# An explicit order list, row-pair projections and a new layout of the casts in a fused attention and mixer kernel

## The chip, the cores and the metric

The kernel runs on one core of one Trainium2 chip. The metric is the device time of one execution in microseconds, given as the median of several runs; the profiler's span of one execution is about 2 us shorter. TensorE does the matmuls and transposes, VectorE and ScalarE the elementwise work, GpSimd some scaling and the issue of transfers that convert types, SyncE the issue of other transfers. Sixteen DMA engines carry all transfers.

## The reference

Linear attention with positive features feeds an MLP mixer. There are 8 batches, 8 heads, 576 tokens of 64 elements per head, 128 features, and mixer widths of 256 (tokens) and 1536 (channels). Cut to what matters:

```python
def phi(x):                                   # x is q or k, scaled
    h = np.einsum('bhsd,md->bhsm', x, omega) - np.sum(x * x, axis=-1, keepdims=True) / 2.0
    return np.exp(h - np.max(h, axis=-1, keepdims=True)) / np.sqrt(m)
q_p, k_p = phi(q_s), phi(k_s)                 # the "projections"
kv = np.einsum('bhsm,bhsd->bhmd', k_p, v)
num = np.einsum('bhsm,bhmd->bhsd', q_p, kv)   # divided by q_p times the sum of k_p: x
h = np.maximum(xt @ w_tok1, 0.0) @ w_tok2     # token mixing; u = x + h
h2 = np.maximum(u @ w_ch1, 0.0) @ w_ch2       # channel mixing; out = u + h2
```

## The kernel before

All operands of the matmuls are fp16 in on-chip memory. TensorE needs q, k and u with their columns on the partitions. For batches 0 and 1, TensorE itself transposes q and k. For batches 2 to 7 the path is longer: a transfer issued by GpSimd casts the fp32 q or k to a scratch array in memory (`cast_dram`), and a DMA transpose issued by SyncE reads it back (`load_T`). The transposes of u are matmuls on TensorE in all batches.

```python
    def cast_dram(b, which):
        src = q if which == "q" else k
        t = dpool.tile([H * SP2, 2 * D], FP16, name=f"{which}16", tag=f"{which}16")
        nc.gpsimd.dma_start(
            out=t.rearrange("(a x) y -> a (x y)", a=P),                     # 128 rows of 4.5 KB
            in_=src[b].rearrange("h (e s) d -> (h e) (s d)", e=P // H),
        )
        live[which + "16", b] = t
    ...
    def q_proj(b, hp, w):          # one of 2 matmuls: all 128 rows, half of them zero in bd
        nc.tensor.matmul(ps, bd[:, w * M : (w + 1) * M], sb[:, 2 * hp : 2 * hp + 2, 0:NP2], ...)
    ...
    def u_transpose(src, dst):     # 4 transposes on TensorE, one copy on VectorE
        ps = mix_ps([P, ND, P], FP16, "uT_ps")
        for db in range(ND):
            nc.tensor.transpose(ps[:, db, :], src[:, db * P : (db + 1) * P], ident16)
        nc.vector.tensor_copy(out=dst, in_=ps)
    ...
    for _, _, fn, args in sorted(steps, key=lambda s: s[:2]):   # order by places in time
        fn(*args)
```

The order of the steps fixes the order on each engine: where one step waits, those behind it on that engine wait too (9.6 us on TensorE in a case below). Each `ps` is a bank of the matmul accumulator (PSUM): three for attention, two for `kv`/`num`, three for the mixer.

The softmax here doesn't subtract the row's maximum and nothing guards it: scores larger than these inputs give would overflow.

Of the kernel before, what the change touches and what calls it, by code (L numbers as in the profile page):

```python
# [17 lines left out]
def kernel(  # L18
# [43 lines left out]
    def att_ps(shape, dt, name):  # L62
        return pspool.tile(shape, dt, name=name, tag="attps", bufs=3)
# [4 lines left out]
    def mix_ps(shape, dt, name):  # L68
        return pspool.tile(shape, dt, name=name, tag="mixps", bufs=3)
# [5 lines left out]

    def cast_dram(b, which):

        src = q if which == "q" else k
        t = dpool.tile([H * SP2, 2 * D], FP16, name=f"{which}16", tag=f"{which}16")
        nc.gpsimd.dma_start(  # L80
            out=t.rearrange("(a x) y -> a (x y)", a=P),
            in_=src[b].rearrange("h (e s) d -> (h e) (s d)", e=P // H),
        )
        live[which + "16", b] = t
# [8 lines left out]
    def load_v(b):  # L93

        if b < 2:
            t = ldpool.tile([P, H, NJ, D], FP16, name="v_16", tag="v_16", bufs=2)
            live["v", b] = t
            nc.gpsimd.dma_start(
                out=t.rearrange("p h j d -> p h (j d)"),
                in_=v[b, :, 0:SM, :].rearrange("h (p j) d -> p h (j d)", j=NJ),  # L100
            )
            return
        t = ldpool.tile([P, H, NJ, D], FP32, name="v_nat", tag="v_nat", bufs=2)
        live["v", b] = t
        for e in range(2):
            nc.sync.dma_start(
                out=t[:, :, 2 * e : 2 * e + 2, :].rearrange("p h w d -> p h (w d)"),
                in_=v[b, :, e * NP2 : (e + 1) * NP2, :].rearrange("h (p w) d -> p h (w d)", w=2),
            )

    def load_v_tail(b):
        t = ldpool.tile([P, 4, D], FP32, name="v_tail", tag="v_tail", bufs=2)
# [27 lines left out]
    def cast_qk(which):  # L140
        nc.vector.tensor_copy(out=live[which + "nat", 0][:, 0:2, :], in_=stage[which])
# [9 lines left out]
    warm = xt[0]  # L151
    nc.vector.memset(warm, 0.0)
    for b in range(2):
        new_nat(b)
# [5 lines left out]
    make_identity(nc, ident16)  # L160
    load_nat(0, 2, 4, "q")
    load_nat(0, 2, 4, "k")
    load_nat(0, 4, 8, "q")
    load_nat(0, 4, 8, "k")
    load_nat_tail(0, "k")
    load_nat_tail(0, "q")
    load_v(0)
# [5 lines left out]
    omega_nat = wpool.tile([P, 2 * D], FP16, name="omega_nat")  # L173
    nc.vector.tensor_copy(out=omega_nat[:, 0:D], in_=om_f)
    nc.vector.tensor_copy(out=omega_nat[:, D : 2 * D], in_=om_f)

    bd = wpool.tile([P, 2 * M], FP16, name="bd")
    nc.vector.memset(bd, 0.0)
# [11 lines left out]

    om_ps = att_ps([P, P], FP16, "om_ps")
# [3 lines left out]

    nc.vector.memset(w1t, 0.0)

    def clear_vz():
        for t in vz:
            nc.vector.memset(t, 0.0)  # L200

    def clear():
        nc.vector.memset(w2t, 0.0)
        nc.vector.memset(xt[1], 0.0)
        for t in q_pt:
            nc.vector.memset(t[:, 0:ST], 0.0)
            nc.vector.memset(t[:, SM + ST : SM + 2 * ST], 0.0)
# [10 lines left out]
    def permute_w2():  # L218
        for tb in range(NT):
            nc.vector.tensor_copy(  # L220
                out=w2m[:, tb], in_=w2raw[:, tb, 0:SM].rearrange("p (c j) -> p j c", j=NJ)
            )
            nc.vector.tensor_copy(out=w2t[:, tb, 0, 0:ST], in_=w2raw[:, tb, SM:S])
            nc.vector.tensor_copy(out=w2t[:, tb, 1, ST:P], in_=w2raw[:, tb, SM:S])
# [15 lines left out]
    steps = []  # L240

    def at(place, fn, *args):
        steps.append((place, len(steps), fn, args))


    def t_main(b, h0, n, which):

        if h0 == 0:
            live[which + "T", b] = ldpool.tile(
                [P, H, SP2], FP16, name=f"{which}T", tag=f"{which}T", bufs=2  # L250
            )
        ps = att_ps([P, n, 2, P], FP16, "t_ps")
# [5 lines left out]
        copy = nc.vector.tensor_copy if which == "q" else nc.scalar.copy  # L258
        copy(  # L259
# [4 lines left out]
    def t_tail(b, which):  # L264
# [4 lines left out]
        nc.vector.tensor_copy(out=live[which + "T", b][:, :, NP2:SP2], in_=ps)  # L269
# [32 lines left out]
    def k_tail_max(b, eng):  # L302
# [8 lines left out]
        for hh in range(4):  # L311
# [3 lines left out]
            eng.tensor_tensor(  # L315
# [6 lines left out]
    def q_proj(b, hp, w):  # L322
        sb = live["qT", b]
        if w == 0:
            live["qp", b, hp] = apool.tile([P, 2, 2, 2, P], FP16, name="q_p", tag="q_p", bufs=3)
        ps = att_ps([P, 2, NP2], FP32, "q_ps")
        nc.tensor.matmul(  # L327
            ps, bd[:, w * M : (w + 1) * M], sb[:, 2 * hp : 2 * hp + 2, 0:NP2], start=True, stop=True
        )
        how = "m i (e p) -> m i e p" if b < 2 else "m i (p e) -> m i e p"  # L330
        exp(live["qp", b, hp][:, w], ps.rearrange(how, e=2))

    def k_proj(b, hp, i):
        sb = live["kT", b]
        if i == 0:
            live["kp", b, hp] = apool.tile([P, 2, 4, M], FP16, name="k_p", tag="k_p", bufs=3)
        ps = att_ps([P, 4, M], FP32, "k_ps")
        for e in range(2):
            nc.tensor.matmul(  # L339
                ps[:, 2 * e : 2 * e + 2, :],  # L340
                sb[:, 2 * hp + i, e * P : (e + 1) * P],
                bd,
                start=True,
                stop=True,
            )
        exp(live["kp", b, hp][:, i], ps)

    def k_max(b, hp, eng):
# [9 lines left out]
        with nc.allow_low_precision(reason="fp16 operand of the matmul"):  # L358
            nc.vector.reciprocal(out=vs[:, :, D], in_=mx)
        eng.tensor_tensor(  # L360
# [6 lines left out]
    def kv(b, hp):  # L367
        ps = kn_ps([P, 2, D + 1], FP32, "kv_ps")
        kp, vs = live["kp", b, hp], live["vsc", b, hp]
        for i in range(2):  # L370
            for j in range(NJ):
                nc.tensor.matmul(  # L372
                    ps[:, i, :], kp[:, i, j, :], vs[:, i * 4 + j, 0 : D + 1], start=(i + j == 0), stop=False
# [11 lines left out]
        nc.scalar.copy(out=sb, in_=ps)  # L385
        live["kv", b, hp] = sb

    def num(b, hp, i):
# [3 lines left out]
        sb = live["kv", b, hp][:, i, :]  # L392
        ps = kn_ps([P, NJ, D + 1], FP32, "num_ps")
# [42 lines left out]
    def tok1(b, tb):  # L436
# [10 lines left out]
        if tb == 0:  # L447
# [29 lines left out]
    def u_transpose(src, dst):  # L477
# [3 lines left out]
        nc.vector.tensor_copy(out=dst, in_=ps)  # L481

    def tokT(b, j):
        if j == 0:
            live["uT", b] = mpool.tile([P, ND, NJ, P], FP16, name="uT", tag="uT")
        u_transpose(live["u", b][:, j, :], live["uT", b][:, :, j, :])
# [39 lines left out]
    L = {"dram2": 1.8, "wc2": 0.001, "dram": 2.766, "T": 2.8, "klo": 1.017, "khi": 3.57, "clo": 4.0, "klo0": 1.094, "khi0": 3.57, "clo0": 4.0, "wc1": 1.85}  # L526
    O = {"qt": -0.334, "kt": 0.472, "ktm": 1.279, "q0": 0.018, "q1": 0.449, "k0": 0.207, "k1": 0.468, "km": 0.711, "kv": 1.426, "num": 1.72, "dn": 0.204, "norm": 1.74, "nt": 2.248}
    O0 = {"qt": 2.914, "kt": 0.685, "ktm": 1.13, "q0": 0.018, "q1": 0.525, "k0": -0.372, "k1": 0.182, "km": 0.711, "kv": 1.426, "num": 1.72, "dn": 0.204, "norm": 1.74, "nt": 2.248, "tq": -0.681, "tk": -0.669, "tail": 0.327}
    O1 = {"qt": 2.914, "kt": 0.685, "ktm": 1.13, "q0": -0.375, "q1": 0.613, "k0": 0.06, "k1": 0.182, "km": 0.711, "kv": 1.426, "num": 1.72, "dn": 0.219, "norm": 1.74, "nt": 2.248, "tq": -0.681, "tk": -0.669, "tail": 0.285}
    def load_second():  # L530
        load_wtok()
        load_nat(1, 0, 4, "q")
        load_nat(1, 0, 4, "k")
        load_nat(1, 4, 8, "q")
        load_nat(1, 4, 8, "k")
        load_nat_tail(1, "k")
        load_nat_tail(1, "q")
        load_v(1)
        load_v_tail(1)

    at(-0.97, cast_qk, "q")
    at(-0.96, cast_qk, "k")
    at(-0.90, load_second)
    at(L["dram2"], cast_dram, 2, "q")
    at(L["dram2"], cast_dram, 2, "k")
    at(L["wc1"], load_wc1, 0)
    at(L["wc1"], load_wc1, 1)
    for part in range(2):
        at(8 + O["kt"] + L["wc2"], load_wc2, part)
    at(0.05, clear_vz)  # L550
    at(0.95, clear)
    at(2.95, permute_w2)
    for b in range(2):
        n = 2 if b == 0 else 4
        o = (O0, O1)[b]
        for h0 in range(0, H, n):
            at(4 * b + h0 / 2 + o["tq"], t_main, b, h0, n, "q")
            at(4 * b + h0 / 2 + o["tk"], t_main, b, h0, n, "k")
        at(4 * b + o["tail"], t_tail, b, "k")
        at(4 * b + o["tail"] + 0.001, t_tail, b, "q")  # L560

    def load_T_v(b):
        for which in "qk":
            load_T(b, which)
        load_v(b)
        load_v_tail(b)

    for b in range(2, B):
        if b > 2:
            for which in "qk":  # L570
                at(4 * (b - 2) + L["dram"], cast_dram, b, which)
        at(4 * (b - 2) + L["T"], load_T_v, b)

    for b in range(B):
        o = (O0, O1)[b] if b < 2 else O
        g = 4 * b
        at(g + o["qt"], q_tail, b)
        at(g + o["kt"], k_tail, b)
        at(g + o["ktm"], k_tail_max, b, nc.gpsimd if b else nc.vector)
        for hp in range(NU):  # L580
            u = g + hp
            at(u + o["q0"], q_proj, b, hp, 0)
            at(u + o["q1"], q_proj, b, hp, 1)
            at(u + o["k0"], k_proj, b, hp, 0)
            at(u + o["k1"], k_proj, b, hp, 1)
# [62 lines left out]
```

## Time and profile before

| | before |
|---|---|
| time, median of 3 runs (range) | 321.0 us (320.54 to 321.78) |
| span of the profiled execution | 318.9 us |
| first channel-mixing matmul | 48.1 us |
| TensorE lost before it / after it | 26.1 us / 2.1 us |
| after the last matmul | 4.8 us |

"Lost" is the time in which TensorE streams nothing that the result needs. The prediction below shows the lines for these. The profile also has the list of DMA issues: how often, how large, and the median time from the issue to the landing in us. For the kernel before:

```profile
q<-in_q_dram POOLq DMA_DIRECT2D x6, 576.0 KB, 7.6
k<-in_k_dram POOLq DMA_DIRECT2D x6, 576.0 KB, 10.2
qT<-q SPq DMA_TRANSPOSE x6, 6.9
```

The first two rows are the six casts of q and of k, the last the six transposes of q.

### The profile page before, as it was taken

The page shows a single profiled execution, that of the slowest core. Times are in us where ns is not written, and L with a number is a line of the kernel's source. Part 1 is how long each engine was busy: PE and PEld are TensorE (multiplying, and loading weights), DVE is VectorE, ACT ScalarE, POOL GpSimd, SP SyncE. Part 2 cuts the span into 40 slices and gives each one's busy share as a digit, 9 for nine tenths or more (in the row PEclk, how much of TensorE's full clock was granted, in tenths as well). Part 3 has the DMA queues.
Part 4 walks back from the last instruction along what each step waited for, and adds up shares of the span by engine and source line. Part 5 has one row for each costly group of instructions (what it writes and reads, how often), then busy time and mean ns, then how long its engine had stood idle before and what let it go on. Part 6 is the DMA issues. An engine that isn't in the chain of part 4 may idle for free.

```text
span 318.9 us, 5525 instructions
## 1 busy us (share of the span) xinstructions
PE 299.3 (94%) x2137; PEld 159.1 (50%) x2137; DVE 173.8 (55%) x463; ACT 155.8 (49%) x299; POOL 71.6 (22%) x102
## 2 busy tenths in 40 slices
PE   5657889999999999999999999999999999999993
PEld 1435455555555555555555555555555444444441
DVE  3599996567455745674558456755385244002011
ACT  1557668633673367416842684358523610440610
POOL 9550535402141214121412131112311000000000
PEclk9598999999999999999999999999999999999998
DMA  7999999999990699059905991110011001002014
GB/s 150 195 195 211 192 244 213 196 238 205 153 256 35 128 173 244 25 123 175 259 3 128 158 238 54 68 66 2 1 67 68 0 27 74 33 2 102 30 39 92
DMA packets 59689, 38.75 MB, mean 121 GB/s; under 512 B 31120, under 2 KB 54544, under 8 KB 59280
## 3 DMA queue, kind: packets, MB, share of 16 engines
q1 hardware_dynamic: 48736, 24.16, 32.4%
q0 software_dynamic: 10656, 13.99, 26.2%
q8 instruction: 16, 0.26, 0.3%
q10 hardware_dynamic: 272, 0.26, 0.3%
q14 instruction: 9, 0.07, 0.1%
HBM read 35.88 MB, written 16.52 MB: 164 GB/s over the span
## 4 chain that ended last, share of the span: by engine, by line
PE 81%; DVE 10%; DMA 3%; POOL 3%; issue 1%; ACT 0%; POOLq 0%; DVEq 0%
PE h_ps L507 29%; PE h_ps L495 28%; PE ht_ps L457 4%; PE k_ps L339 3%; PE q_ps L327 3%; PE h_ps L441 3%; DMA v<-in_v_dram 3%; PE uT_ps L480 2%; PE num_ps L396 2%; PE kv_ps L372 2%; DVE xm L405 1%; PE kv_ps L377 1%; DVE km L355 1%; PE htt_ps L468 1%; POOL vz L315 1%
## 5 line engine op out<-in xcount | busy, mean ns | idle before, releaser
L507 PE MATMUL h_ps<-wc,r 128*128 128x512 f16 x432 | 98.1, 379 | 0.0
L502 ACT ACTIVATE r<-h_ps 128x512 f16<-128x512 f32 x108 | 64.8, 600 | 58.4 <-PE h_ps L495 56.2
L495 PE MATMUL h_ps<-uT,wc 128*128 128x512 f16 x384 | 93.0, 379 | 0.2 <-DVE uT L481 0.2
L507 PEld LDWEIGHTS <-r 128*128 128x128 f16 x432 | 41.0, 98 | 45.8
L495 PEld LDWEIGHTS <-wc 128*128 128x128 f16 x432 | 40.9, 98 | 41.3 <-issue 0.5
L360 POOL TENSOR_TENSOR v_sc<-v_nat,v_sc 128x512 f16<-128x512 f32 x24 | 25.4, 1058 | 130.5 <-DVE rc L404 91.4
L272 ACT ACTIVATE q_p<-q_ps 128x512 f16<-128x512 f32 x64 | 38.0, 599 | 33.1 <-PE q_ps L327 33.0
L516 DVE TENSOR_TENSOR o_sb<-um,h_ps 128x512 f32<-128x512 f16 x32 | 22.0, 688 | 48.0 <-PE h_ps L507 47.6
L272 ACT ACTIVATE k_p<-k_ps 128x512 f16<-128x512 f32 x64 | 37.8, 598 | 2.8 <-PE k_ps L339 1.5
L351 DVE TENSOR_TENSOR mx<-k_p 128x512 f16<-128x512 f16 x32 | 13.6, 425 | 37.0 <-ACT k_p L272 37.0
L405 DVE TENSOR_TENSOR xm<-num_ps,rc 128x256 f16<-128x256 f32 x64 | 27.1, 424 | 2.2
L385 ACT CAST kv_sb<-kv_ps 128x130 f16<-128x130 f32 x32 | 8.5, 266 | 39.1 <-PE kv_ps L377 39.0
L327 PE MATMUL q_ps<-qT,bd 128*128 128x512 f16 x64 | 24.9, 395 | 1.6 <-DVE qT L259 1.6
L339 PE MATMUL k_ps<-bd,kT 128*128 128x256 f16 x128 | 25.1, 282 | 0.9 <-ACT kT L259 0.9
L460 DVE TENSOR_TENSOR um<-xm,ht_ps 128x512 f16<-128x512 f16 x32 | 21.7, 683 | 4.0 <-PE ht_ps L457 3.9
L355 DVE TENSOR_REDUCE km<-mx 128x8 f16<-128x512 f16 x32 | 21.9, 686 | 1.1
L396 PEld LDWEIGHTS <-q_p 128*128 128x128 f16 x256 | 16.0, 99 | 10.5 <-issue 0.3
L315 POOL TENSOR_TENSOR vz<-v_tail,vz 32x256 f16<-32x256 f32 x28 | 17.3, 616 | 17.0 <-DVE vz L314 15.4
L457 PE MATMUL ht_ps<-r,w2m 128*128 128x512 f16 x64 | 19.0, 379 | 0.2
L396 PE MATMUL num_ps<-kv_sb,q_p 128*128 128x65 f16 x256 | 17.9, 195 | 0.1
L339 PEld LDWEIGHTS <-kT 128*128 128x128 f16 x128 | 12.1, 100 | 10.6 <-ACT kT L259 1.7
L441 PE MATMUL h_ps<-xm,w1m 128*128 128x512 f16 x64 | 16.4, 379 | 0.0
(93 smaller groups left out, 270.7 us busy)
## 6 DMA issues: line engine op xcount, KB each, us to landing
out_dram<-o_sb SPq DMA_DIRECT2D x32, 256.0 KB, 2.4
v_nat<-in_v_dram SPq DMA_DIRECT2D x12, 512.0 KB, 5.7
q<-in_q_dram POOLq DMA_DIRECT2D x6, 576.0 KB, 7.6
k<-in_k_dram POOLq DMA_DIRECT2D x6, 576.0 KB, 10.2
wc<-in_moe_w_ch_dram POOLq DMA_DIRECT2D x4, 768.0 KB, 14.9
v_tail<-in_v_dram SPq DMA_DIRECT2D x32, 32.0 KB, 4.7
v<-in_v_dram POOLq DMA_DIRECT2D x2, 512.0 KB, 8.6
out_dram<-o_sb SPq DMA_DIRECT2D x8, 128.0 KB, 2.3
```

What stands on the lines that cost most here:

```text
L272: nc.scalar.activation(out=out, in_=in_, func=AF.Exp, bias=0.0, scale=c_scale)
L327: nc.tensor.matmul(ps, bd[:, w * M : (w + 1) * M], sb[:, 2 * hp : 2 * hp + 2, 0:NP2], start=True, stop=True)
L339: nc.tensor.matmul(ps[:, 2 * e : 2 * e + 2, :], sb[:, 2 * hp + i, e * P : (e + 1) * P], bd, start=True, stop=True,)
L355: nc.vector.reduce_max(out=mx, in_=tmp, axis=AX.X)
L360: eng.tensor_tensor(out=vs[:, :, 0:D], in0=live["v", b][:, 2 * hp : 2 * hp + 2].rearrange("p h j d -> p (h j) d"), in1=vs[:, :, D : D + 1] ...
L396: nc.tensor.matmul(ps[:, j, :], live["qp", b, hp][:, j % 2, i, j // 2, :], sb, start=True, stop=True)
L405: nc.vector.tensor_tensor(out=live["x", b][:, :, h * D : (h + 1) * D], in0=ps[:, :, 0:D], in1=rc.unsqueeze(2).broadcast_to((P, NJ, D)), op ...
L441: nc.tensor.matmul(ps, w1m[:, j, tb * P : (tb + 1) * P], live["x", b][:, j, :], start=(j == 0), stop=False)
L457: nc.tensor.matmul(ps, w2m[:, tb, j, :], live["r1", b][:, tb, :], start=(tb == 0), stop=(tb == NT - 1))
L495: nc.tensor.matmul(ps, wc1[:, db, cb * P : (cb + 1) * P], uT[:, db].rearrange("p j c -> p (j c)"), start=(db == 0), stop=(db == ND - 1),)
L502: nc.scalar.activation(out=live["r3", c][:, cb, :], in_=ps, func=AF.Relu)
L507: nc.tensor.matmul(ps, live["r3", c][:, cb, j * P : (j + 1) * P], wc2[:, cb, :], start=(cb == 0), stop=(cb == NCB - 1),)
```

## The change

The stated intent: one explicit order list for all steps, weights ahead of batch 2, the first channel chunk moved up, row-pair projections, zero matmuls in early gaps. The diff, cut to its core:

```diff
     def att_ps(shape, dt, name):
-        return pspool.tile(shape, dt, name=name, tag="attps", bufs=3)
+        return pspool.tile(shape, dt, name=name, tag="attps", bufs=4)
     def mix_ps(shape, dt, name):
-        return pspool.tile(shape, dt, name=name, tag="mixps", bufs=3)
+        return pspool.tile(shape, dt, name=name, tag="mixps", bufs=2)
+    HEAT = {('kv', 0, 0): 3, ('kv', 0, 1): 2, ... }      # cut: 49 zero matmuls in 16 places
 # ... cut: SWAP, which moves some copies between VectorE and ScalarE
     def cast_dram(b, which):
-            out=t.rearrange("(a x) y -> a (x y)", a=P),
-            in_=src[b].rearrange("h (e s) d -> (h e) (s d)", e=P // H),
+            out=t.rearrange("(a n x) y -> n a (x y)", a=4 * H, n=9),
+            in_=src[b].rearrange("h (e n s) d -> n (h e) (s d)", e=4, n=9),
+    def heat(ps, *key):
+        for _ in range(HEAT.get(key, 0)):
+            nc.tensor.matmul(ps, warm[:, 0:P], warm, start=True, stop=True)
 # ... cut: order of the first loads; w2's permutation and tail scaling to GpSimd
-    def q_proj(b, hp, w): ...
-    def k_proj(b, hp, i): ...
+    def proj(b, hp):
+        rows = [slice(w * D, (w + 1) * D) for w in range(2)]
+        om = [bd[rows[w], w * M : (w + 1) * M] for w in range(2)]
+        heat(kps[0], "proj", b, hp)
+        for t in range(4):
+            for w in range(2):
+                nc.tensor.matmul(kps[w][:, t, :],
+                    kT[rows[w], 2 * hp + t // 2, (t % 2) * P : (t % 2 + 1) * P], om[w], ...)
+        for w in range(2):
+            nc.tensor.matmul(qps[w], om[w], qT[rows[w], 2 * hp : 2 * hp + 2, 0:NP2], ...)
+    def u_write(b, j):          # u of batches 2 to 7 and the tails to memory
+        nc.sync.dma_start(out=live["u16", b][j * P : (j + 1) * P, :], in_=src)
+    def load_uT(b):             # and back, transposed
+        for db in range(ND):
+            nc.sync.dma_start_transpose(out=dst[:, db]..., in_=live["u16", b][:, db * P : (db + 1) * P])
-    L = {"dram2": 1.8, ... }    # cut: all places in time and the sort over them
+    order = """
+        load_nat_tail 1 k; load_nat 1 0 4 k; load_nat 1 0 4 q; cast_qk k; cast_qk q; t_main 0 0 2 k; ...
+        num_tail 0 0; t_main 1 4 4 k; permute_w2 0; kv 0 3; num 0 3 1; load_T_v 2; proj 1 1; ...
+        1; t_main 1 4 4 q; norm 0 3 0; load_v_all 2; num_tail 0 1; tok1 0 0; ...
+    """                         # cut: 81 lines
```

One part of the diff is in no word of the intent: the layout of the casts. The scratch array holds the same bytes afterwards, but the transfer now goes over 9 groups of 32 pieces of 2 KB, with the 9 outermost, where it went over 128 pieces. (Another edit that no word names: the tail of v has one buffer in place of two. SyncE waits up to 8.9 us for it after the change, but also 9.4 us in the fastest kernel of the study, so it isn't what separates them.)

## The prediction

> **What bounds the kernel now.** I read the page's busy shares first, then the span in slices, then the busy time per stretch, then the chain that ended last, and at the end the TensorE groups by shape. The page, parts 1 and 2:
>
> ```profile
> span 318.9 us, 5525 instructions
> ...
> PE 299.3 (94%) x2137; PEld 159.1 (50%) x2137; DVE 173.8 (55%) x463; ACT 155.8 (49%) x299; POOL 71.6 (22%) x102
> ...
> PE   5657889999999999999999999999999999999993
> ...
> DVE  3599996567455745674558456755385244002011
> ...
> PEclk9598999999999999999999999999999999999998
> DMA  7999999999990699059905991110011001002014
> ```
>
> One slice is 8 us. TensorE is full from the seventh slice (48 us) to the end. Before that it is not, its clock dips twice, VectorE is the full engine and the DMA engines are full too. The busy time per stretch (columns: stretch, length, busy PE, PEld, DVE, ACT, POOL, each with its count, then granted clock, DMA share and GB/s) says the same in numbers:
>
> ```profile
> 10.00:20.00 10.00, 5.72 (x58) 3.61 (x57) 7.18 (x26) 5.40 (x11) 5.57 (x8) 0.71 1.39 198
> 20.00:30.00 10.00, 7.49 (x84) 5.18 (x85) 9.55 (x29) 7.07 (x14) 2.07 (x4) 0.83 1.37 222
> 40.00:50.00 10.00, 8.80 (x89) 5.29 (x87) 9.43 (x26) 6.78 (x14) 2.72 (x5) 1.00 1.18 250
> 90.00:120.00 30.00, 30.00 (x222) 16.32 (x221) 17.99 (x48) 15.88 (x32) 6.97 (x11) 1.00 0.65 145
> ```
>
> So there are two stages. Up to about 48 us VectorE is the bound (9.4 to 9.6 of 10 us) on data that is still arriving; after it TensorE has no hole at all and nothing but fewer TensorE cycles helps. The chain in order of time (start, length, what) gives the pitch of a stream of matmuls and both ends of the second stage:
>
> ```profile
> 39.81 0.44 PE k_ps L339 x4
> 46.62 0.40 PE uT_ps L480 x4
> 47.27 0.77 DVE uT L481 x2
> 48.08 1.02 PE h_ps L495 x4
> ...
> 272.63 10.36 PE h_ps L495 x48
> ...
> 314.11 0.69 DVE o_sb L516
> ```
>
> 48 matmuls in 10.36 us is 0.216 us for one of 512 columns, though the group list shows 379 ns for it (its end includes the pipeline's drain). Start to start in the trace, back to back, I find 0.216 (512 columns), 0.109 (256), 0.0555 (128), 0.058 (130) and 0.030 us (65). Multiplying each group's count by its pitch gives the work that TensorE must stream: 287.6 us, of which 1.7 is warming. The 285.9 us left, with 4.8 us after the last matmul (314.1 to 318.9), leave 28.2 us lost. The first channel matmul starts at 48.1 us, and the list of instructions has 22.0 us of useful streaming before it: 26.1 us are lost there, 2.1 us in the remaining 266 us.
>
> **What the Trainium skill says.** Row pairs: "TensorE: Matmul & The Clock Gate", Part 3, says that matmuls on different row groups run concurrently in the array, and gives 3.07 times for four; "TensorEngine Tiling (Array Packing)", Gotcha 1, adds that row tiles must write different PSUM banks, which explains why the change gives each half its own bank. The trace before has no paired tiles, so it can't confirm it. The same tiling page, Key Properties, says that changing the tiling mode drains TensorE. Here the trace has something: the 32-row transposes of the tails. Weight loads in the timeline:
>
> ```profile
> 30.43 0.24 PEld L268 LDWEIGHTS <-natt 32*128 32x128 f16 x7 [0.22 <-issue]
> 30.70 0.10 PEld L372 LDWEIGHTS <-k_p 128*128 128x128 f16 x1
> ```
>
> The seven 32-row loads follow each other every 0.025 us; the last starts at about 30.58, and the next load, of 128 rows, only at 30.70. It agrees: about 0.1 us for a switch. On the clock, the first page, Part 1, says that idling about one window of 3.4 us halves the clock; the records here show half clock at 9.0 to 15.9 and 22.7 to 26.1 us, a multiple of that window, so I believe that filler matmuls can hold it.
>
> **The change, part by part.**
>
> *Projections.* 64 query matmuls of 512 columns and 128 key matmuls of 256 become 64 of 512 and 256 of 128, on 64 rows each, in pairs.
>
> ```profile
> L339 PE MATMUL k_ps<-bd,kT 128*128 128x256 f16 x128 | 25.1, 282 | 0.9 <-ACT kT L259 0.9
> L327 PE MATMUL q_ps<-qT,bd 128*128 128x512 f16 x64 | 24.9, 395 | 1.6 <-DVE qT L259 1.6
> L480 PE MATMUL uT_ps<-ident,um 128*128 128x128 f16 x128 | 12.2, 219 | 0.8 <-DVE um L460 0.6
> ```
>
> Before: 64 x 0.216 + 128 x 0.109 = 27.8 us. After, if a pair costs one: 32 x 0.216 + 128 x 0.0555 = 14.0 us. Saved: 13.8. Against it, each of the 32 groups enters and leaves the 64-row mode: 2 x 0.1 us, 6.4 us in all; the eight groups of batches 0 and 1 lie mostly in gaps, so I charge 24 of them, 4.8 us. For imperfect overlap inside pairs I choose 1.5 us (0.05 a group).
>
> *Transposes of u.* 144 before, 32 after (batches 0 and 1 only); the others go to memory and come back by DMA transposes. Saved on TensorE: 112 x 0.0555 = 6.2 us. VectorE also loses 28 copies.
>
> So the streaming work after is 285.9 - 13.8 - 6.2 + 4.8 + 1.5 = 272.2 us.
>
> *The early stage.* I summed VectorE's and ScalarE's work ahead of the first channel chunk from the two instruction lists with the durations of the trace. VectorE: about 42 us before; after about 31 (batch 0's tail scaling, half its v scaling and the w2 permutation go to GpSimd, several copies to ScalarE, memsets into its idle start). ScalarE: at most 29 before (busy time up to 50 us), after about 33, because it takes those copies and the chunk is preceded by the same exponentials (0.60 us each). The full engine thus changes: 33 us of ScalarE from about 5.5 us (first data) at the 86% that VectorE reached before ((42 - 6) / (48 - 6), an estimate) is 44 us, and in front of the first channel chunk stand only 18.2 us of useful streaming (projections are cheaper): 25.8 us lost. At 95% it would be 40.2 and 22.0. I choose 24.5, a gain of 1.6 us. The 49 zero matmuls (10.6 us at full clock) fill gaps, and I count nothing for them beyond the held clock that these numbers need.
>
> *Loads.* Before, batch 0 and the token weights are the first 2.06 MB (fp16 bytes, by shape) of GpSimd's queue. After, batch 1's q and k and half of w_ch1 are queued ahead of the token weights: 3.96 MB, which the rate of the trace (this queue's packets bring 0.2 MB per us from about 5 us on) has in at about 26 us. The first token matmul can't run before that, and by ScalarE's sum not before about 33. It should be hidden.
>
> *PSUM.* Projections get four banks, the mixer falls from three to two. ScalarE starts 0.42 us after the start of a channel chunk's last matmul and takes 0.60; the same bank is wanted 1.08 us after that start if three chunks follow each other. The slack is 0.06 us, so each exponential that stands before such an eviction can stall TensorE for up to 0.6. The order list spreads the chunks between other matmuls; ScalarE has 44 us for 40 us of TensorE work at the beginning, but only 4 to 8 per 8 us later. I choose 4 us for all later stalls, against 2.1 before.
>
> Sum: 24.5 lost early + 272.2 + 4 + 4.8 after the last matmul = 305.5 us of span. The time is 2.1 us above the span before (321.0 against 318.9): 307.6. I shade it to 306, since the order list looks fitted to such waits.
>
> **Rivals.**
> 1. *The pairs do not overlap.* For it: the trace before shows no such pair, and both halves need their own weight load, which must then load beside the other half's matmul. Against: the skill's measured figure. It gives back 13.8 - 1.5: about 318, within 2%.
> 2. *ScalarE or the two mixer banks become the bound later.* For it: 0.06 us of slack, and TensorE's time per batch shrinks while the exponentials do not. Against: 173 us of ScalarE in all, about 57% of the new span. With 0.3 us lost at each of 30 chunks, 9 us instead of 4: 311.
> 3. *The way through memory is too slow.* A write landed in 2.4 us before, a large transpose held the queue for 3.1 and landed in 6 to 7. I expect 8 us from the last token matmul to the transposed tile. The list leaves 12.3 to 23 us of TensorE work there. It should be hidden. Batch 5's q and k have the thinnest margin: 12.4 us of work from the cast to the first use, where the cast took 5 to 12 before. One such miss costs 3 us: 309.
> 4. *The early stage gains more*, with ScalarE near 95% full: 303; and mode switches hidden as well: 299.
>
> **Range and chances.** All good terms together give 298, rivals 2 and 3 together 314. I take 298 to 315 for 8 in 10. Faster by over 2% needs a time below 314.6; only the pairs failing, or two rivals at once, prevent it: 0.86. Within 2%: 0.13. Slower: 0.01.
>
> **What would show it.** Right: the projection pairs start a few ns apart, 128-column key pairs at a pitch near 0.056 us; u's transposes fall to 32; the first channel matmul near 42 us; the clock at 1.00 from about 8 us on; TensorE idle after 50 us below 5 us. Wrong: key halves at 0.0555 each in turn (pairs serial); gaps well over 0.1 us at the edges of a projection; TensorE waiting for the relu of a channel chunk, or for DMA transposes of u, q or k; the first channel matmul still at 48 us.

## The result, and the profile after

| | before | after |
|---|---|---|
| time, median (range), 4 runs each | 320.77 us (320.40 to 321.78) | 337.85 us (336.16 to 338.84) |
| span of the profiled execution | 318.9 us | 334.4 us |
| mean granted clock | 0.980 | 0.968 |
| first channel-mixing matmul | 48.1 us | 45.3 us |

The change made the kernel 5.2% slower: the ratio is 1.0522, with a 95% interval of 1.0469 to 1.0575. Here and below a ratio is the mean time of one kernel's fast runs over that of the other's fast runs of the same rounds, so not quite the ratio of the medians quoted. Executions over 1.5% slower than the fastest of the same kernel are left out of the means.

The page after, parts 1 and 2 (busy time and share of each engine; then tenths busy in 40 slices, of 8.4 us here):

```profile
span 334.4 us, 5703 instructions
...
PE 300.0 (90%) x2202; PEld 147.7 (44%) x2202; DVE 160.6 (48%) x418; ACT 157.6 (47%) x305; POOL 81.3 (24%) x115
...
PE   6897999809999079999999999999999999999994
...
PEclk9999999976999669999999999999999999999999
```

The first six slices are better filled than before, and from the sixteenth on the row is full, as before. What is new are two holes in the row of TensorE, in the ninth and the fourteenth slice, and a lower clock in and after each. In the time per stretch (same columns as in the prediction) they are plain:

```profile
60.00:70.00 10.00, 6.01 (x26) 2.43 (x25) 6.00 (x14) 1.83 (x4) 0.00 (x0) 1.00 1.28 183
70.00:80.00 10.00, 5.03 (x53) 3.75 (x53) 1.99 (x6) 1.65 (x5) 4.49 (x6) 0.54 0.62 139
90.00:120.00 30.00, 20.18 (x159) 9.93 (x156) 13.94 (x38) 13.54 (x28) 7.32 (x10) 0.86 1.03 126
```

The stretch of 90 to 120 us was the one with 30.00 us of TensorE before; now it has 20.18. GpSimd did nothing from 60 to 70 us, and in the 5 us from 67 to 72 the four compute engines together were busy for 0.04 us, which points at a transfer. The view of waits names it (engine, line waited at, releaser: us in total, times, longest):

```profile
PE qt_ps L281 <- DMA qT<-q: 10.8, 3, 9.6
PE kv_ps L388 <- POOL v_sc L374: 7.8, 2, 7.0
```

TensorE waits 9.6 us for one DMA transpose of q. The 7.0 us wait for GpSimd is a transfer too: GpSimd's own row in the timeline shows that it waited for v of batch 2.

```profile
72.19 2.07 POOL L374 TENSOR_TENSOR v_sc<-v_nat,v_sc 128x512 f16<-128x512 f32 x2 [17.72 <-DMA v_nat<-in_v_dram]
```

The chain that ended last, in order of time (start, length, what), has these transfers as its longest pieces, and its shares by engine changed from 81% TensorE and 3% DMA to 60% and 24%:

```profile
52.87 20.11 DMA v_tail<-in_v_dram
...
100.02 18.65 DMA qT<-q
...
137.41 12.51 DMA qT<-q
```

And the rows of the DMA issues that answer to those of before:

```profile
q<-in_q_dram POOLq DMA_DIRECT2D x6, 576.0 KB, 11.7
k<-in_k_dram POOLq DMA_DIRECT2D x6, 576.0 KB, 13.0
qT<-q SPq DMA_TRANSPOSE x6, 10.3
```

A cast of q takes 11.7 us where it took 7.6, a transpose of q 10.3 where it took 6.9. Same bytes, same number.

I made a count of TensorE's gaps for all kernels: the time by which the start of each matmul lies later than the pitch of the one before it allows, if that is over 50 ns. It is 24.3 us before and 46.1 after. Up to 50 us it fell (22.4 to 13.0, with the zero matmuls counted as work); the rest is 11.6 us at 60 to 82 us, 11.3 at 108 to 123, and about 10 elsewhere.

### The profile page after: what moved, and what is told of

It is laid out like the page before. It is cut to its first block, busy times and chain, and to the rows that moved or that the text cites. A ratio compares the mean times of both kernels' runs of the same rounds, so it can differ in the third digit from the quotient of the medians.

```text
span 334.4 us, 5703 instructions
## 1 busy us (share of the span) xinstructions
PE 300.0 (90%) x2202; PEld 147.7 (44%) x2202; DVE 160.6 (48%) x418; ACT 157.6 (47%) x305; POOL 81.3 (24%) x115
## 4 chain that ended last, share of the span: by engine, by line
PE 60%; DMA 24%; DVE 4%; SPq 4%; POOL 3%; ACT 3%; issue 1%; POOLq 0%; DVEq 0%
PE h_ps L542 23%; PE h_ps L530 20%; DMA qT<-q 11%; DMA v_tail<-in_v_dram 7%; DMA v<-in_v_dram 4%; PE ht_ps L475 3%; SPq L124 2%; PE h_ps L459 2%; PE k_ps L338 2%; PE num_ps L414 2%; PE kv_ps L388 2%; DMA natt<-in_k_dram 1%; PE q_ps L346 1%; SPq L115 1%; POOL vz L318 1%
## 5 line engine op out<-in xcount | busy, mean ns | idle before, releaser
L542 PE MATMUL h_ps<-wc,r 128*128 128x512 f16 x432 | 97.1, 379 | 0.2 <-ACT r L537 0.2
L530 PE MATMUL h_ps<-uT,wc 128*128 128x512 f16 x384 | 94.1, 381 | 0.6 <-DVE rc L422 0.4
L530 PEld LDWEIGHTS <-wc 128*128 128x128 f16 x432 | 39.9, 98 | 43.3 <-issue 4.0
L551 DVE TENSOR_TENSOR o_sb<-um,h_ps 128x512 f32<-128x512 f16 x32 | 21.9, 686 | 49.4 <-PE h_ps L542 49.3
L275 ACT ACTIVATE q_p<-q_ps 128x512 f16<-128x512 f32 x64 | 36.8, 603 | 17.8 <-PE q_ps L346 17.8
L423 DVE TENSOR_TENSOR xm<-num_ps,rc 128x256 f16<-128x256 f32 x64 | 27.2, 425 | 2.2
L318 POOL TENSOR_TENSOR vz<-v_tail,vz 32x256 f16<-32x256 f32 x32 | 20.0, 623 | 29.1 <-DVE vz L317 14.3
L422 DVE RECIPROCAL rc<-num_ps 128x4 f32<-128x4 f32 x64 | 10.9, 171 | 23.5 <-PE num_ps L414 23.3
L475 PE MATMUL ht_ps<-r,w2m 128*128 128x512 f16 x64 | 20.2, 403 | 0.6 <-ACT r L537 0.5
L388 PE MATMUL kv_ps<-v_sc,k_p 128*128 128x65 f16 x256 | 13.5, 196 | 7.9 <-POOL v_sc L374 7.8
L414 PEld LDWEIGHTS <-q_p 128*128 128x128 f16 x256 | 14.9, 100 | 11.9 <-issue 3.2
L388 PEld LDWEIGHTS <-k_p 128*128 128x128 f16 x256 | 12.1, 100 | 16.1 <-issue 9.6
## 6 DMA issues: line engine op xcount, KB each, us to landing
q<-in_q_dram POOLq DMA_DIRECT2D x6, 576.0 KB, 11.7
```

Source lines behind the costliest of these rows:

```text
L275: nc.scalar.activation(out=out, in_=in_, func=AF.Exp, bias=0.0, scale=c_scale)
L318: nc.gpsimd.tensor_tensor(out=vs[r, hh, :, 0:D], in0=live["vt", b][r], in1=vs[r, hh, :, D : D + 1].broadcast_to((32, 4, D)), op=ALU.mult,)
L388: nc.tensor.matmul(ps[:, i, :], kp[:, j % 2, 2 * i + j // 2, :], vs[:, i * 4 + j, 0 : D + 1], start=(i + j == 0), stop=False)
L414: nc.tensor.matmul(ps[:, j, :], live["qp", b, hp][:, j % 2, i, j // 2, :], sb, start=True, stop=True)
L423: nc.vector.tensor_tensor(out=live["x", b][:, :, h * D : (h + 1) * D], in0=ps[:, :, 0:D], in1=rc.unsqueeze(2).broadcast_to((P, NJ, D)), op ...
L475: nc.tensor.matmul(ps, w2m[:, tb, j, :], live["r1", b][:, tb, :], start=(tb == 0), stop=(tb == NT - 1))
```

## The experiments

The theory: the casts in the new layout take longer, the transfers behind and beside them (the transposes on SyncE's queue and v behind those) land late, and TensorE waits for them. The rivals: the order list issues something in a wrong place (v of batch 2, casts of batches 4 and 5); the pairs do not overlap; the zero matmuls or the way of u through memory cost time. In all these runs the outputs were correct, and the kernel before took 320.7 to 321.1 us (medians).

### The old layout in the changed kernel

```diff
-            out=t.rearrange("(a n x) y -> n a (x y)", a=4 * H, n=9),
-            in_=src[b].rearrange("h (e n s) d -> n (h e) (s d)", e=4, n=9),
+            out=t.rearrange("(a x) y -> a (x y)", a=P),
+            in_=src[b].rearrange("h (e s) d -> (h e) (s d)", e=P // H),
```

> The changed kernel with the casts of q and k to memory in the layout of before (packets of 18 KB in place of 2 KB), nothing else. If the small packets of the new layout made casts and DMA transposes slow beside each other, the landing of qT of batch 4 (18.65 us from 100.0 us on) falls below 12 us and the time falls by some 10 us to about 328. If what matters is only that a cast is in flight beside a transpose or a load on the hardware queue, the stalls at 66 and 109 us stay within 3 us and the time stays at 335 to 341; larger packets could even make the small ones of the transposes wait longer.

Measured: 314.37 us (312.05 to 317.48), ratio 0.9765 (0.9707 to 0.9823). These two lines alone are worth 23 us, over twice what I expected. TensorE's waits for qT fell from 10.8 to 2.5 us, and the wait for v of batch 2 is gone:

```profile
PE qt_ps L281 <- DMA qT<-q: 2.5, 1, 2.5
```

The run changes the size of the pieces together with their grouping; the runs with 16 and 12 groups below part the two. Since the interval reaches across 0.98, faster by 2% is not settled by this run.

### The new layout in the kernel before

```diff
-            out=t.rearrange("(a x) y -> a (x y)", a=P),
-            in_=src[b].rearrange("h (e s) d -> (h e) (s d)", e=P // H),
+            out=t.rearrange("(a n x) y -> n a (x y)", a=4 * H, n=9),
+            in_=src[b].rearrange("h (e n s) d -> n (h e) (s d)", e=4, n=9),
```

> The kernel before with only the new layout of the casts (9 x 32 rows of 1024 elements). If the layout alone makes casts hold part of the DMA engines for long, before also gets slower: the casts' landing rises from 7.6 and 10.2 us to over 12, TensorE gets waits for qT or kT after 50 us, and the time rises by 5 to 20 us, to 326 to 341. If the layout hurts only together with the changed order and the extra DMA transposes of u, before stays within 2% (below 327).

Measured: 336.08 us (334.73 to 336.77), ratio 1.0476 (1.0443 to 1.0508). The layout slows the old kernel by about as much as the whole change did, with the same kinds of waits:

```profile
PE kv_ps L372 <- POOL v_sc L360: 6.5, 1, 6.5
PE k_ps L339 <- DMA kT<-k: 3.1, 1, 3.1
```

So the layout needs neither the order list nor anything else of the change to do its harm. It is the cause of the loss; the rest of the change, by the run before, gains.

### The number of outermost groups: 16 and 12 instead of 9

The pieces stay at 2 KB and every byte goes where it went; only the number of groups changes.

```diff
-            out=t.rearrange("(a n x) y -> n a (x y)", a=4 * H, n=9),
-            in_=src[b].rearrange("h (e n s) d -> n (h e) (s d)", e=4, n=9),
+            out=t.rearrange("(a n x) y -> n a (x y)", n=16, x=8),      # 12 in the other run
+            in_=src[b].rearrange("h s d -> (h s) d").rearrange("(a n s) d -> n a (s d)", n=16, s=16),
```

> The changed kernel with casts of the same 2 KB packets, but the outermost dimension of the copy is 16 in place of 9 (16 x 18 x 1024). If what hurts is that an outermost dimension of 9 leaves part of the 16 DMA engines out, this is as good as the old layout: 312 to 318. If what hurts is the small packets, it stays at 330 to 340.

> The changed kernel with the casts' outermost dimension 12 (12 x 24 x 1024), packets of 2 KB as with 9 and 16. If the outermost dimension sets how many of the 16 DMA engines a cast uses, the busy sum of the DMA engines during a cast alone is about 12 (it was 8 to 10 with 9 and 16 to 18 with 16), and the time lies between 310.5 and 337.9, at 313 to 326. If only a multiple of 16 helps and everything else is as bad as 9: 330 or more.

Measured with 16: 310.45 us (309.90 to 311.29), ratio 0.9685 (0.9654 to 0.9715), the fastest kernel. With 12: 327.14 us (323.32 to 331.03), ratio 1.0095 (1.0065 to 1.0125) from its two fast runs of 323.32 and 324.31; its profile fell on one of the two slow ones. The order 9, 12, 16 gives the ratios 1.0522, 1.0095, 0.9685.

The packets in the trace show why. Adding up the durations of all packets of the casts in stretches of 1 us in which little else runs gives the mean number of engines at work for a cast alone: 6.3 to 10.0 with 9 groups (93 to 98 us of that run), 12.4 to 13.2 with 12 (up to 14.5 later in the run), 16.6 to 17.9 with 16 (over 16 because packets overlap), and 16.1 to 16.2 in the kernel before. A packet of 2 KB took 172 to 173 ns (median) in all three layouts, so the packets are not slower; fewer run side by side. In bytes that is 74 to 104 KB per us with 9 groups and 154 to 203 with 16.

The records hold two more signs of it. First, GpSimd's queue has 3248 packets of 4 bytes with 9 groups, 1712 with 12 and 560 with 16. Per cast that is 224 and 96 more than with 16, just 7 x 32 and 4 x 24: one for each piece on each engine that the groups leave out. Second, two casts issued back to back fill the engines and then leave a tail. In the kernel before with the new layout each later pair of casts ran on 16 to 18 engines (by the same sum) for some 5 us and then on about 2.2 for some 4 us more (97 to 100 us, 129 to 133 and so on). This fits an estimate: two casts of nine shares each over 16 engines leave two engines with a second share, and 32 packets of 172 ns take 5.5 us. No record names the engine, so that they are the same two is inferred.

The profile of the kernel with 16 groups, the same stretches as above:

```profile
60.00:70.00 10.00, 9.62 (x98) 5.26 (x97) 9.30 (x24) 3.83 (x9) 3.47 (x5) 1.00 1.12 195
70.00:80.00 10.00, 10.00 (x78) 5.08 (x77) 5.66 (x16) 4.25 (x9) 3.07 (x4) 1.00 0.76 206
```

The hole is closed and the clock stays at 1.00. Its casts land in 8.0 and 8.3 us:

```profile
q<-in_q_dram POOLq DMA_DIRECT2D x6, 576.0 KB, 8.0
k<-in_k_dram POOLq DMA_DIRECT2D x6, 576.0 KB, 8.3
```

Longer casts would do less harm if other transfers ran at full speed beside them. They don't. In the changed kernel about two engines (1.9) were at work on casts at 109 to 112 us, and the packets of the transposes beside them took 204 to 215 ns on the mean, 85 to 104 of them per us. At 113 us, in a pause of the cast (112.5 to 113.8 us), they took 18 ns and 1022 came in one us; at 116 to 119 us, beside seven engines of the cast, they were back at 143 to 154 ns. Beside another such tail at 70 to 72 us none began at all, and the 18 in flight took 3.2 to 3.4 us each.

That a badly spread cast slows the transposes more than a well spread one is not shown. What differs plainly is how long they meet: after 18 us, DMA transposes ran beside at least one engine's worth of GpSimd's transfers for some 35 us in the changed kernel, and for 6 us with 16 groups. Why two engines hold up sixteen, these runs do not show.

### Mending by the order list: v of batch 2 earlier, casts of batch 4 and 5 closer together

```diff
-  ... num 0 3 1; load_T_v 2; proj 1 1; ... norm 0 3 0; load_v_all 2; num_tail 0 1; ...
+  ... num 0 3 1; load_T 2 q; load_v_all 2; load_T 2 k; proj 1 1; ... norm 0 3 0; num_tail 0 1; ...
```

> The changed kernel with batch 2's v loads issued between the two DMA transposes of batch 2 (at about 42.7 us, where the DMA moves only 81 GB/s) in place of behind both (48.5 us, together with w_ch2 and the casts of batch 3). Collision theory: v and its tail land before 60 us, the wait of TensorE at 66 us (7.1 + 1.9 us) and the half-clock stretch at 70.9 us go, time down by 9 to 13 us, to 325 to 329. Rival, that the DMA engines are simply short of bytes at that stage: another load (kT of batch 2, w_ch2) comes late instead and TensorE waits for that, time unchanged within 3 us.

Measured: 338.95 us (337.10 to 343.42), ratio 1.0544. The wait moved and grew, as the rival said. (The 81 GB/s in the expectation I find in no view. From 42.7 to 48.5 us the trace has 103 GB/s at a DMA share of 1.26, so few bytes moved, but the engines were not free.) The waits of TensorE:

```profile
PE k_ps L338 <- DMA kT<-k: 11.2, 1, 11.2
PE qt_ps L281 <- DMA qT<-q: 10.2, 3, 8.9
```

v now comes in time, k of batch 2 does not, and TensorE waits for it from 52.9 to 64.1 us. The second edit:

```diff
-  ... num 2 2 0; cast_dram 4 q; num 2 3 0; ... k_max 3 0; cast_dram 4 k; num_tail 2 1; ...
+  ... num 2 2 0; cast_dram 4 q; cast_dram 4 k; num 2 3 0; ... k_max 3 0; num_tail 2 1; ...
-  ... kv 3 0; cast_dram 5 q; proj_exp 3 1 0; ... proj 4 1; cast_dram 5 k; ...
+  ... kv 3 0; proj_exp 3 1 0; ... proj 4 1; cast_dram 5 q; cast_dram 5 k; ...
```

> The changed kernel with the cast of k of batch 4 issued right behind that of q, and that of q of batch 5 moved later, next to that of k. Collision theory: no cast is in flight beside the transposes of batch 4, qT of batch 4 lands in under 8 us in place of 18.65, the wait at 108.8 us (9.7 us) shrinks below 3 us with its half-clock stretch, time down by 7 to 12 us, to 326 to 331. If the transposes are slow for another reason (their number, the write-backs), the wait stays above 7 us.

Measured: 331.79 us (330.07 to 333.07), ratio 1.0337. The 9.6 us wait at 109 us is gone, but waits of 4.4 us at 138 and 2.4 at 209 came, and that for v of batch 2 stayed (6.6 us). Of the 17 us lost, this edit brings 6. Order was a partial remedy for the second hole, no cause: with the layout mended, both places in the list are harmless as they stand.

### The pairs, alone

```diff
-        rows = [slice(w * D, (w + 1) * D) for w in range(2)]
+        rows = [slice(0, P) for w in range(2)]
```

With this the two halves use all 128 rows (zeros in one half of the weights) and run one after the other, in the same order list. It was run on the changed kernel and, later, on the kernel with 16 groups.

> The changed kernel with every projection matmul on all 128 rows (the zero half of the block-diagonal omega included), so neither pairs nor a change of tiling mode; order, banks and all else as changed. If pairs run concurrently and a switch costs 0.1 us: TensorE's streaming grows by 13.8 us and the switches' 6.4 go, so up to 7 us slower where TensorE is the bound, less while it waits for DMA: 339 to 346. If the pairs are what slows the changed kernel (mode switches, bank conflicts), it gets faster, below 334.

> The changed kernel with the casts' outermost dimension 16 (310.45 us) and every projection matmul on all 128 rows: no pairs, no change of tiling mode. If pairs run concurrently and a switch costs about 0.1 us as predicted, this is slower by 13.8 - 6.4 = 7 us or a little more: 316 to 320. If the switches eat the gain: within 2 us of 310.5.

Measured: 341.36 us (339.91 to 342.06), ratio 1.0632, against 1.0522 of the changed kernel; on the mended one 315.81 us (315.05 to 316.13), ratio 0.9842 (0.9821 to 0.9863), against 0.9685. The pairs are worth 5.4 us by the medians (5.0 by the ratios) where TensorE is the bound, 3.5 where it waits for transfers anyway. The timeline of the changed kernel shows one projection of each kind, and that they overlap:

```profile
97.62 0.40 PE L338 MATMUL k_ps<-bd,kT 64*128 64x128 f16 x8
97.85 0.38 PE L346 MATMUL q_ps<-qT,bd 64*128 64x512 f16 x2
98.17 0.20 PE L414 MATMUL num_ps<-kv_sb,q_p 128*128 128x65 f16 x1
```

From the first of eight key matmuls of 128 columns to the query matmuls it is 0.23 us (one after the other, at the pitch of 0.0555, 0.44), and the two query matmuls of 512 take 0.32 together with the change of mode. In single records the second of a pair starts 3 ns after the first; the next instruction starts 305 to 309 ns later, 216 of streaming and about 90 of switching. The same is lost on the way in: with 16 groups the first key matmul of each of the 24 projections after 50 us starts 93 to 97 ns later than the pitch allows, without pairs 0 to 3 ns. So 0.1 us for a switch, at both ends, was well predicted.

### The zero matmuls, alone

```diff
-    HEAT = {('kv', 0, 0): 3, ('kv', 0, 1): 2, ... }
+    HEAT = {}
```

This was run on the changed kernel with the old layout. A second run, on the kernel with 16 groups, took `HEAT.get(key, 0) // 2` matmuls in each place, 20 of 49.

> The changed kernel with the old cast layout and without the 49 zero matmuls. If the fillers only fill gaps and hold the clock, taking them out brings half-clock stretches back before 45 us and costs 0 to 5 us (314 to 319). If they stand in the way of useful matmuls (10.6 us of streaming ahead of the first channel chunk), the time falls by 2 to 6 us (308 to 312).

> The changed kernel with the casts' outermost dimension 16 and 20 of the 49 zero matmuls (half of each group, rounded down). With all 49 the clock holds but the fillers are part of the chain that ends last; with none (on the old cast layout) the clock halves and the time was the same within 1 us. If the clock holds with 20 as well, 29 x 0.216 = 6.3 us of fillers go, of which part was hidden: 306 to 309. If the clock falls, 309 to 312.

Measured without any: 313.52 us (311.62 to 314.82), ratio 0.9773, against 0.9765 with them. With 20: 313.22 us (310.99 to 322.52, one slow run in six), ratio 0.9703 (0.9678 to 0.9728), against 0.9685 (0.9654 to 0.9715). Neither is a clear difference. With 20 the clock held (no half clock before 98 us), so I had expected 306 to 309; the five fast runs have a median of 312.6, and why is open. The clock they do hold; without any its row is:

```profile
PEclk9575699999997999999999999999999999999998
```

Half clock was granted at 9.1 to 19.3 and 22.7 to 36.4 us there, with about 19 us of gaps up to 50 us against 12.6 with the zero matmuls. Yet the first channel matmul came at 43.99 us without them and at 44.77 with them. In the chain of the kernel with 16 groups they are 25% of the stretch from 18 to 47 us, because real work stands behind them in TensorE's order:

```profile
20.95 1.62 PE heat_ps L166 x7
```

So what the held clock gained, the zero matmuls seem to have taken.

### The transposes of u, back on TensorE

First on the changed kernel with the old layout, with `tokT` (four transposes) in the places of `u_write`; batch 3's at the place of `load_uT`, since I judged that earlier places would end in a deadlock; no such build was run. Then on the kernel with 16 groups, all in the places of `load_uT`, where the result is needed later:

```diff
-  ... num 3 0 1; u_write 2 0; tok2 2 2; ... num 3 2 1; load_uT 2; norm 3 2 1; ...
+  ... num 3 0 1; tok2 2 2; ... num 3 2 1; tokT 2 0; tokT 2 1; tokT 2 2; tokT 2 3; norm 3 2 1; ...
```

> The changed kernel with the old cast layout and u transposed on TensorE for all batches, as before (batch 3's four transposes stand where its tile was loaded back). By the pitch, 112 transposes cost 6.2 us on TensorE and 28 copies go back to VectorE: 319 to 323 if the way through memory is hidden and free. If the way through memory costs DMA time that TensorE waits for (qT of batch 4 and 5), the two cancel: 310 to 316.

> The changed kernel with the casts' outermost dimension 16, u transposed on TensorE for all batches as before, but each batch's four transposes placed where the tile was loaded back in the list, some 6 us of TensorE work or more after the last add into u, so that they wait for no add. If u_on_PE cost 20 us only because the transposes stood right behind the adds, this costs the transposes themselves and their evictions: 112 x 0.0555 = 6.2 us, 316 to 320. If the way through memory saves more than its TensorE time (mixer banks, VectorE), 325 or more. If the DMA transposes of u cost TensorE something by contention, 310 to 315.

Measured: 334.25 us (333.84 to 334.89), ratio 1.0426, in the first form, 19.9 us above its base; 326.62 us (324.32 to 327.13), ratio 1.0166, in the second, 16.2 us above its base. For the first form I had expected 5 to 9 us at the most, for the second 6 to 10 or, if the banks mattered, 15 and more; the latter came true. Gaps account for the rest: 39.1 against 25.2 us in the first form, 31.4 against 21.5 in the second. 6.2 + 9.9 is 16.1. In the first form the longest waits at the transposes are for the adds that make u (5.3 us in all); in the second no such wait is left. The timeline of the second form:

```profile
133.50 0.39 PE L498 MATMUL uT_ps<-ident,um 128*128 128x128 f16 x4
134.35 0.61 PE L498 MATMUL uT_ps<-ident,um 128*128 128x128 f16 x8 [0.46 <-ACT r L540]
135.25 0.38 PE L498 MATMUL uT_ps<-ident,um 128*128 128x128 f16 x4 [0.29 <-DVE uT L499]
```

Four transposes use up a mixer bank in 0.22 us, and the next four wait until ScalarE or VectorE has emptied one. The view of waits gives such waits at the transposes 4.6 us, and by the count of gaps 7.6 us lie there. So the way through memory spares TensorE waits as well as the transposes. That three banks would remove them was not run. This is the price in this order list with two mixer banks; an order made for transposes on TensorE might make it smaller, and was not tried.

## Why the prediction was wrong, point by point

**The step that failed is the term "I choose 4 us for all later stalls", with the landing times of the casts under rival 3.** For transfers, only rival 3 could add to that term: "the cast took 5 to 12 before. One such miss costs 3 us: 309." That was the cast of the kernel before. I carried it over to the kernel after, without seeing that the diff rewrites the access pattern of that very transfer. The casts then took up to 19.0 us, and 30.1 us were lost after the first channel matmul: one miss of 9.6 us (qT of batch 4), one of 7.0 (v of batch 2) and several of 0.5 to 2. Batch 5, which I thought the thinnest, cost 0.5. The Trainium skill would have warned me: "DMA: Bandwidth & Descriptors", Rules for kernel authors, row "Use all 16 engines", says that an outermost dimension of a size c under 16 confines a transfer to at most c engines. The traces agree for a cast alone: about 8 engines at work with 9 groups, 13 with 12, 17 with 16. The prediction cites no page for the casts. What rival 3 says of u itself held: the view of waits has none of TensorE for a transposed tile of u.

The sum shows where the 28.9 us between the predicted span of 305.5 and the measured 334.4 lie:

| term | predicted, us | changed kernel | with 16 groups |
|---|---|---|---|
| lost before the first channel matmul | 24.5 | 27.1 | 26.7 |
| lost after it | 4 | 30.1 | 5.0 |
| after the last matmul | 4.8 | 4.9 | 4.9 |
| span | 305.5 | 334.4 | 308.7 |

The second row is worked out with my predicted streaming: 272.2 in all, 18.2 of it before the first channel matmul, so 254.0 after. In the changed kernel that matmul starts at 45.33 us and the last ends at 329.47, which leaves 284.1 - 254.0 = 30.1. In the kernel with 16 groups it is 44.85 and 303.8, so 5.0. Nearly all of the error (26.1 of 28.9 us) is in this one row, and the layout of the casts takes 25 us of it away.

**Projections, right in kind, a little short in size.** The pairs overlap, and rival 1 falls. The projections take 20.9 us from start to start (8.0 for k, 12.9 for q with the switch back), and the switches into the mode, 32 of about 0.095 us by the measured ones, another 3.0: 23.9, where I had 14.0 + 6.4 + 1.5 = 21.9. The difference of 2.0 lies in the early stage, where five pairs of query matmuls start 0.13 to 0.84 us apart. The net worth without pairs and with them was 5.4 us, where I had 13.8 - 4.8 - 1.5 = 7.5.

**Transposes of u, too small.** I counted the 6.2 us of streaming alone. Put back, they cost 16 to 20 us in this order, with waits for the adds in the first form and for mixer banks in the second. Waits for the two banks were in rival 2, but I applied them to the channel chunks and not to what the change had taken away. This does not mean that the change gained 16 us: before, with three banks and its own order, these transposes caused hardly any wait (2.1 us lost in all after 48 us).

**The early stage, only partly right.** VectorE stopped being the bound, and the first channel matmul came earlier, but at 45.3 us and not at 42. "The full engine thus changes" to ScalarE is wrong: ScalarE is busy 27.2 us up to then, not 33, so 68% of the 39.8 us from 5.5 us on. No engine is full with needed work there. "Loads" was right for what it named: w1m landed at 26.2 us, as predicted, and was first used at 34.8. But v of batch 1 stands behind it. The chain goes from engine to engine, and in the changed kernel it holds one piece of 13.03 us, the load of v for batch 1, which is issued at 22.96 us behind the weights. With 16 groups the first channel matmul is still at 44.85, so this load is not the whole reason.

**Zero matmuls, counted as nothing: right.** They hold the clock that the other numbers assumed, and take about as much time themselves.

**Later stalls and the end, right with the layout mended.** 5.0 us lost against 4, and 4.9 after the last matmul against 4.8. The first is partly luck: the 4 us were meant for matmuls that wait for the relu of a chunk, and the view of waits shows only 0.7 us of these after the first channel matmul. With 16 groups the kernel takes 310.45 us, inside the range of 298 to 315 that was meant for the changed kernel.

What stays open is why the packets of the transposes stretch while a cast is at work on only some engines, and why the first channel matmul does not come before about 44 us in any of the kernels.

## What to carry to other kernels

Read the access pattern of every transfer in a diff, even of those that the change's description leaves out, and compare the size of its outermost dimension with the 16 engines: a size of 16 here was worth 27 us over a size of 9. Times of transfers may be carried from one profile to another only if the pattern and what runs beside it stay the same. When a change with several parts comes out slower, undo the part that feeds the longest wait first, and put that part alone into the old kernel: the two runs together settled this.

## What the Trainium skill lacked or had wrong

- "DMA: Bandwidth & Descriptors", the row "Use all 16 engines": right, and it gives no number for the cost. Here 9, 12 and 16 groups of equal 2 KB pieces kept about 8, 13 and 17 engines at work when a cast ran alone, and the ratios to the kernel before were 1.0522, 1.0095 and 0.9685.
- No page that I read says what a badly spread cast does to DMA transposes beside it: their packets took 204 to 215 ns instead of 18 while casts were at work on about two engines.
- "TensorEngine Tiling (Array Packing)", Key Properties, says that a change of mode drains TensorE, and gives no time: about 0.09 us at each end of a projection here.
- "TensorE: Matmul & The Clock Gate", Part 1, says that the clock halves after a window of about 3.4 us without work. Here less was enough: in the kernel without zero matmuls half clock began at 9.1 and 22.7 us, after 3.4 us in which TensorE, by starts and pitches, had streamed for 1.4 and 1.7 us. With the zero matmuls no half clock came before 70 us. What the page does not warn of is that such fillers stand ahead of real work in TensorE's order: 313.52 us without them, 314.37 with them, no gain.
